# More tensor work released per unit in the second batch, a normalisation moved from VectorE to GpSimd, 7 instead of 14 leading products

## Chip, cores and metric

The kernel runs on one core of a Trainium2 chip. The metric is the device time of one execution in microseconds (us); the time of a kernel is the median of its runs. The core's engines run side by side and each works through its own list of instructions in order: TensorE (PE in the rows; PEld is its weight load), VectorE (DVE), ScalarE (ACT), GpSimd (POOL), and SyncE (SP), which here issues nearly all transfers.

## What is computed

Three layers in a row, on 2 batches of 576 tokens: attention with 8 heads of 64 that keeps, for each query, the 32 largest scores; a gated MLP; a mixture of 8 experts.

```python
scores = q @ k.T / 8                                   # per head, 576 x 576
attn = softmax(scores where >= 32nd largest) @ v       # -> x, 576 x 512 per batch
h = gelu(x @ w_in);  u, vv = halves(h)                 # 512 columns each
v_n = (vv - mean(vv)) / sqrt(var(vv) + 1e-6) * g_ln    # per token
x = x + (u * (w_sg @ v_n + b_sg)) @ w_out              # w_sg mixes the 576 tokens
# router: expert e of a token is the argmax of x @ w_gate, or the expert of the token before
out = p[e] * (relu(x @ w1[e]) @ w2[e])
```

The line that the change touches is `(vv - mean) / sqrt(var)`: one value normalisation per tile of tokens.

## The kernel before

**Units.** Attention works in units of 128 queries of one head (the 64 left over of a batch are paired into half as many units), 36 per batch, 72 in all. Line numbers are those of the profile. A unit is: scores on TensorE (L325) and their copy to `s_sb` on ScalarE (L328); on VectorE the 24 largest by segments (L354, L357, L359, the last 8 into `last`); a sign mask and its count on ScalarE (L365) and a product on GpSimd into `rest` (L369, L370), of which VectorE takes the next 8 (`next`, L371); the exponential on ScalarE (L367, with `nm` from GpSimd, L362); the mask on VectorE (L381) or, every second unit, on ScalarE and GpSimd (L378, L379); five transposes on TensorE (L393, `pt_ps`), their copy `pt` on ScalarE (L396); the product with v on TensorE (L401, `pv`), and after every fourth unit the division into the tile's `row` on VectorE (L406, L408, L417).

**The rest of the work** is cut into steps in a queue named `between`, each with an estimate in us. The function `pump` is called after each unit with a number from the table `RATE` (one entry per tile, 5 for each batch): it adds that number to a credit (at most 6) and takes steps off the queue, in order, while the credit lasts. Steps are: loading and decoding `w_in` (8 of 2.0, L196 to L204); per tile of tokens the MLP's input, 8.1 in all (L453 for u, L459 for v, L566 for the router's share); then for the first batch `spread` (20 in all, L541), `load_projection` (14; its first four steps are decoding of `w_out` and hold no product), `decide` (4.4) and `project` (14.4, L617). These last four, and the MLP of the tile shared by both batches, are queued when the second batch's first tile is done; the MLP of each tile of the second batch is queued behind them when that tile is done. When the last unit is done, `x_done` transposes the last tile (L439, copied to `xT` by ScalarE, L440), what is left on the queue is emptied, and the last tile's MLP, the second batch's `spread` (L523), the router and the experts follow.

**The order.** The kernel is written in a framework whose scheduler places every instruction by priority and by a model of time. Units have a high priority, so they run ahead of the queue's steps as far as buffers allow (7 of `s_sb`, 5 of `e_sb`). A change in the number or cost of instructions therefore moves others on all engines.

**The normalisation** (L470 to L477, once for each of 9 tiles): ScalarE writes the gelu of v into a `row` buffer (L466), VectorE takes its mean and variance (L470, L472) and adds 1e-6 (L474), GpSimd raises that to the power -0.5 (L476), and VectorE writes (v - mean) times that into `vn` (L477). Of the second batch's `vn`, ScalarE writes a high part and GpSimd the rest (L490, L491), both of which the products of L523 read.

**The start.** 14 products of constants (L821, `WARM`) that nothing reads lead TensorE's list, before the first scores.

Of the kernel before, what the change touches and what calls it, by code (L numbers as in the profile page):

```python
# [17 lines left out]
OP = mybir.AluOpType  # L18
# [4 lines left out]

WIDTHS = (224, 176, 160, 152, 152, 144, 136, 120)

RATE = (2.0, 2.0, 2.0, 2.0, 2.0, 2.4, 2.4, 2.4, 2.2, 2.2)

AHEAD = 2000
EVAC = 2000
# [7 lines left out]

FILL = (2, 2, 2, 3)

WARM = 14  # L40
KEEP = 30


# [1 line left out]
def tile_topk_gmlp_moe(  # L45
# [15 lines left out]
    nc = tc.nc  # L61
# [107 lines left out]
    def attention(fast):  # L169
# [76 lines left out]
        KK, QH, QL, V1, XB, XT, VN, UT, LG, DONE = {}, {}, {}, {}, {}, {}, {}, {}, {}, []  # L246

        def load_k(b, h):
            if PLAIN[b]:
                if h % 2 == 0:  # L250
                    KK[b, h] = kv.tile([P, S], F32R, name="kk", bufs=8).bitcast(F32)
                    nc.sync.dma_start(KK[b, h], kT[b, h:h + 2].rearrange("h d s -> (h d) s"))
                return
            kr = raw.tile([P, S], F32, name="kr")
            for s in range(2):
                nc.sync.dma_start(kr[s * D:(s + 1) * D], kT[b, h])
            KK[b, h] = kv.tile([P, S], F32R, name="kk", bufs=8)
            nc.scalar.activation(KK[b, h], kr, AF.Copy)
            nc.gpsimd.tensor_tensor(KK[b, h][D:], kr[D:], KK[b, h][D:].bitcast(F32), op=OP.subtract)
# [163 lines left out]
        def tile_of(b, j):  # L423
            return (b, j) if j < NJ - 1 else BOTH
# [17 lines left out]
        def mlp_in(t):  # L442
            b, j = t
            ps = {}

            def u(f):
                if f == 0:
                    if j == 0 or t == BOTH:
                        VN[b] = one.tile([P, 1 if t == BOTH else NJ - 1, F2], F32, name="vn2" if t == BOTH else "vn")
                        UT[b] = one.tile([P, CF, P if t == BOTH else FULL], F32, name="ut2" if t == BOTH else "ut")  # L450
                    ps["u"] = ps_m.tile([P, CF, P], F32, name="m_ps")
                for c in range(CD):
                    nc.tensor.matmul(ps["u"][:, f, :], w_in_sb[:, c, f * P:(f + 1) * P], XT[t][:, c, :], start=c == 0,  # L453
                                     stop=c == CD - 1)

            def v(c):
                if c == 0:
                    ps["v"] = ps_m.tile([P, F2], F32, name="m_ps")
                nc.tensor.matmul(ps["v"], XT[t][:, c, :], w_in_sb[:, c, F2:], start=c == 0, stop=c == CD - 1)  # L459
                if c < CD - 1:  # L460
                    return
                DONE.append(t)
                k = j % (NJ - 1)
                with tc.high_priority(offset=EVAC):
                    vg = one.tile([P, F2], F32, name="row", bufs=3)
                    gelu = nc.scalar.activation(vg, ps["v"], AF.Gelu_apprx_tanh)  # L466
                    with tc.issue_after(gelu.ins):
                        nc.scalar.activation(UT[b][:, :, k * P:(k + 1) * P], ps["u"], AF.Gelu_apprx_tanh)
                    st = sm.tile([P, 6], F32, name="st", bufs=3)
                    nc.vector.bn_stats(st, vg)  # L470
                    mv = sm.tile([P, 2], F32, name="mv", bufs=3)
                    nc.vector.bn_aggr(mv, st)  # L472
                    ve = sm.tile([P, 1], F32, name="ve", bufs=3)
                    nc.vector.tensor_scalar(ve, mv[:, 1:2], 1e-6, None, op0=OP.add)  # L474
                    rs = sm.tile([P, 1], F32, name="rs", bufs=3)
                    nc.gpsimd.tensor_tensor(rs, ve, neghalf, op=OP.pow)  # L476
                    nc.vector.tensor_scalar(VN[b][:, k, :], vg, mv[:, 0:1], rs, op0=OP.subtract, op1=OP.mult)  # L477

            return ([(0.9, partial(u, f)) for f in range(CF)] + [(0.9, partial(v, c)) for c in range(CD)]
                    + [(0.9, partial(logits_x, t))])  # L480

# [270 lines left out]
        def pump(us):  # L752
            credit[0] = min(credit[0] + us, 6.0)
            while between and credit[0] >= between[0][0]:
                cost, step = between.pop(0)
                credit[0] -= cost
                with tc.issue_after(BACK[-1].ins), tc.issue_after(EVACS[-1].ins):
                    step()

        def body(b, fast):  # L760
            for m, j in enumerate(TILES[b]):
# [3 lines left out]
                for i in range(n):  # L765
# [11 lines left out]
                    if fast and b + 1 < B and m == NJ - 1:  # L777
                        with tc.high_priority(offset=1):
                            for h in range(2 * i + 1, min(2 * i + 3, H)):
                                load_k(b + 1, h)  # L780
                    pump(RATE[b * NJ + m] if fast else 100.0)
                t = tile_of(b, j)
# [27 lines left out]
        def begin(b):  # L810
            for h in range(H):
                if h % 4 == 0:
                    load_q(b, TILES[b][0], h)
                load_k(b, h)
                if h == H - 1:
                    load_v(b)


        idle = ps_m.tile([P, 4, P], F32, name="m_ps")
        for m in range(WARM):  # L820
            nc.tensor.matmul(idle, ones, tri[:, None, :].to_broadcast([P, 4, P]), start=m == 0, stop=m == WARM - 1)  # L821
        begin(0)
# [336 lines left out]
```

## Time and profile before

| what | us |
|---|---|
| median of 3 runs | 582.87 (582.1 to 584.3) |
| the profiled execution, whole time | 582.34 |
| its span (first to last instruction) | 580.5 |
| TensorE busy | 521.7 (90%) |
| VectorE busy | 335.2 (58%) |
| ScalarE busy | 297.0 (51%) |
| GpSimd busy | 258.0 (44%) |

The profiled execution took 1.8 us more than its span and 0.5 us less than the median. Busy shares are means over stages with different limits: attention of the first batch runs to about 185 us, that of the second to 356 us, the experts from about 429 us to the end, and each stage has to be read by itself. In a row of the timeline the first number is the start, the second how long it took, both in us; what stands in brackets at a row's end is the idle time of the engine before it, and what ended it.

### The profile page before, as it was taken

To read this page: it belongs to the slowest core of one execution; us is meant where nothing else is said; L and a number is where in the kernel's file an instruction comes from. 1 tells how busy PE (TensorE), PEld (TensorE's weight loads), DVE (VectorE), ACT (ScalarE), POOL (GpSimd) and SP (SyncE) were. 2 spreads that over 40 slices of the span, in tenths; PEclk is the share of its full clock that TensorE was granted. 3 is DMA by queue.
4 is the path that set the end of the run, shared out by engine and by line. 5 is a ranking of instruction groups with operands and counts; after the bars stand their busy time and mean duration, and the time that the engine had idled before them with its cause. 6 is when DMAs were issued, how large, how long until landed. Compare 5 with 4: busy or idle time off the path is not lost. (4 is left out here: it accounts for less than half of the span.)

```text
span 580.5 us, 10259 instructions
## 1 busy us (share of the span) xinstructions
PE 521.7 (90%) x3414; PEld 442.7 (76%) x3414; DVE 335.2 (58%) x1626; ACT 297.0 (51%) x545; POOL 258.0 (44%) x382
## 2 busy tenths in 40 slices
PE   6566898989989799998999999989889999999993
PEld 3445686867868587887866787786579999999992
DVE  4789998969789798689998711266301111111110
ACT  3579888979787887479877432321010111011110
POOL 5497997657758475447676510520310101000010
PEclk9799899999999999999999999999999999999997
DMA  8962320000000000003101300002599997684000
GB/s 173 268 191 81 112 72 5 25 1 28 20 10 28 19 16 5 11 20 92 46 29 36 110 20 19 0 1 74 186 356 387 389 376 264 234 297 169 18 36 17
DMA packets 42609, 61.55 MB, mean 106 GB/s; under 512 B 14056, under 2 KB 18152, under 8 KB 42544
## 3 DMA queue, kind: packets, MB, share of 16 engines
q1 hardware_dynamic: 40880, 55.80, 29.5%
q0 software_dynamic: 1664, 4.97, 2.5%
q8 instruction: 30, 0.49, 0.4%
q14 instruction: 35, 0.29, 0.2%
HBM read 53.68 MB, written 7.33 MB: 105 GB/s over the span
## 5 line engine op out<-in xcount | busy, mean ns | idle before, releaser
L401 PE MATMUL pv<-v,pt 128*128 128x128 f32 (+1 forms) x720 | 104.7, 279 | 7.3 <-DVE row L417 4.8
L401 PEld LDWEIGHTS pv<-v,pt 128*128 128x128 f32 x720 | 96.2, 194 | 15.1 <-DVE row L417 5.5
L369 POOL TENSOR_TENSOR rest<-s_sb,sg 128x576 f32<-128x576 f32 x72 | 93.3, 1296 | 28.5 <-ACT sg L365 27.2
L325 PE MATMUL s_ps<-kk,qh 128*128 128x288 f32 x288 | 86.2, 423 | 16.0 <-ACT s_sb L328 15.0
L354 DVE MAX8 cand<-s_sb 128x8 f32<-128x72 f32 x576 | 88.7, 219 | 13.7 <-ACT s_sb L328 13.5
L393 PE MATMUL pt_ps<-ident,e_sb 128*128 128x128 f32 x360 | 68.1, 277 | 16.3 <-ACT pt L396 5.5
L995 PE MATMUL h_ps<-xw,w_sb 128*128 128x152 f32 (+6 forms) x512 | 76.5, 298 | 1.0 <-DMA w_sb<-in_w_dram 1.0
L1006 PE MATMUL y_ps<-hT,w_sb 128*128 128x152 f32 (+6 forms) x512 | 75.3, 299 | 0.9 <-DMA w_sb<-in_w_dram 0.9
L325 PEld LDWEIGHTS s_ps<-kk,qh 128*128 128x128 f32 x288 | 50.2, 194 | 31.3 <-ACT s_sb L328 21.4
L995 PEld LDWEIGHTS h_ps<-xw,w_sb 128*128 128x128 f32 x512 | 71.4, 190 | 1.3 <-ACT hT L998 1.3
L1006 PEld LDWEIGHTS y_ps<-hT,w_sb 128*128 128x128 f32 x512 | 71.0, 190 | 1.2 <-DMA w_sb<-in_w_dram 1.2
L396 ACT ACTIVATE pt<-pt_ps 128x640 f32<-128x640 f32 x72 | 50.3, 699 | 36.3 <-PE pt_ps L393 36.1
L998 ACT ACTIVATE hT<-h_ps 128x152 f32<-128x152 f32 (+6 forms) x32 | 9.7, 302 | 113.1 <-PE h_ps L995 109.9
L393 PEld LDWEIGHTS pt_ps<-ident,e_sb 128*128 128x128 f32 x360 | 45.2, 143 | 28.2 <-ACT pt L396 8.3
L365 ACT ACTIVATE sg<-s_sb,last 128x576 bf16<-128x576 f32 x72 | 55.6, 773 | 18.7 <-DVE last L357 15.4
L371 DVE MAX8 next<-rest 128x8 f32<-128x583 f32 x72 | 54.7, 759 | 8.2 <-POOL rest L370 8.0
L367 ACT ACTIVATE e_sb<-s_sb,nm 128x576 f32<-128x576 f32 x72 | 55.5, 772 | 1.9 <-POOL nm L362 1.7
L967 POOL DMA_INDIRECT out_dram<-orow,to x10 | 10.0, 999 | 103.1 <-ACT orow L966 48.3
L328 ACT ACTIVATE s_sb<-s_ps 128x576 f32<-128x576 f32 x72 | 46.3, 642 | 13.3 <-PE s_ps L325 12.8
L1000 DVE TENSOR_SCALAR hT<-h_ps 128x152 f32<-128x152 f32 (+6 forms) x32 | 10.3, 323 | 73.6 <-PE h_ps L995 68.6
L379 POOL TENSOR_TENSOR e_sb<-e_sb,mask 128x576 f32<-128x576 f32 x36 | 46.3, 1287 | 13.4 <-ACT e_sb L367 6.7
L1008 DVE COPY yT<-y_ps 128x152 f32<-128x152 f32 (+6 forms) x32 | 9.9, 323 | 64.2 <-PE y_ps L1006 64.2
(247 smaller groups left out, 827.2 us busy)
## 6 DMA issues: line engine op xcount, KB each, us to landing
w_sb<-in_w_dram SPq DMA_DIRECT2D x32, 1024.0 KB, 12.4
dbl<-in_w_in_dram SPq DMA_DIRECT2D x8, 512.0 KB, 4.5
kk<-in_kT_dram SPq DMA_DIRECT2D x8, 288.0 KB, 4.9
qh<-in_qT_dram SPq DMA_DIRECT2D x32, 64.0 KB, 2.4
v<-in_v_dram SPq DMA_DIRECT2D x8, 256.0 KB, 6.1
dbl<-in_w_out_dram SPq DMA_DIRECT2D x4, 512.0 KB, 3.7
xin<-row SPq DMA_DIRECT2D x8, 256.0 KB, 2.0
back<-xin SPq DMA_DIRECT2D x8, 256.0 KB, 2.6
```

What stands on the lines that cost most here:

```text
L325: nc.tensor.matmul(s_ps[:, n, :HS], w, k[:, n * HS:(n + 1) * HS], start=m == 0, stop=m == len(terms) - 1)
L328: EVACS.append(nc.scalar.activation(s_sb.rearrange("p (n s) -> p n s", n=2), s_ps[:, :, :HS], AF.Copy))
L354: nc.vector.max(cand[:, 8 * g:8 * g + 8], s_sb[:, g * w:(g + 1) * w])
L365: nc.scalar.activation(sg, s_sb, AF.Sign, bias=last8[:, un, 7:8], scale=-LESS, accum_out=cnt)
L367: nc.scalar.activation(e_sb, s_sb, AF.Exp, bias=nm, scale=scale)
L369: nc.gpsimd.tensor_tensor(below[:, :S], s_sb, sg, op=OP.mult)
L371: nc.vector.max(next8[:, un, :], below)
L393: tr = nc.tensor.transpose(pt_ps[:, t * P:(t + 1) * P], p_sb[:, k0:k0 + P], ident)
L396: nc.scalar.activation(pt.rearrange("p t q -> p (t q)"), pt_ps[:, :NJ * P], AF.Relu)
L401: nc.tensor.matmul(PV[b][:, i % g, :], pt[:, t, :], V1[b][:, t, w * i * (D + 1):w * i * (D + 1) + nv], start=t == 0, stop=t == NJ - 1)
L995: nc.tensor.matmul(hp[:, :W], w1_sb[:, c, f * P:(f + 1) * P], xw[:, c, at], start=c == 0, stop=c == CD - 1)
L1006: nc.tensor.matmul(yp[:, :W], w2_sb[:, f, c * P:(c + 1) * P], hT[:, f, :W], start=f == 0, stop=f == CE - 1)
```

## The change

```diff
-RATE = (2.0, 2.0, 2.0, 2.0, 2.0, 2.4, 2.4, 2.4, 2.2, 2.2)
+RATE = (2.0, 2.0, 2.0, 2.0, 2.0, 2.8, 2.8, 2.8, 2.6, 2.6)
-WARM = 14
+WARM = 7
                     nc.gpsimd.tensor_tensor(rs, ve, neghalf, op=OP.pow)
-                    nc.vector.tensor_scalar(VN[b][:, k, :], vg, mv[:, 0:1], rs, op0=OP.subtract, op1=OP.mult)
+                    nc.gpsimd.tensor_scalar(VN[b][:, k, :], vg, mv[:, 0:1], rs, op0=OP.subtract, op1=OP.mult)
```

The last five entries of `RATE` belong to the second batch. Seven products leave TensorE's list, and nine normalisations go from VectorE's list to GpSimd's. The scheduler then places everything anew; three places show it.

VectorE near the start, before: the rows from the last maximum of the second unit on. L199 and L200 decode a piece of `w_in` that a transfer brings into `dbl`.

```order
L357 MAX last<-cand 128x8
L199 TENSOR_SCALAR m_ps<-dbl 128x512
L359 MATCH_REPLACE cand<-ta,cand 128x64
L354 MAX cand<-s_sb 128x8 x4
L371 MAX next<-rest 128x8
L354 MAX cand<-s_sb 128x8 x4
L200 SCALAR_TENSOR_TENSOR m_ps<-dbl,m_ps 128x512
L357 MAX ta<-cand 128x8
L199 TENSOR_SCALAR m_ps<-dbl 128x512
L381 SCALAR_TENSOR_TENSOR e_sb<-s_sb,next,e_sb 128x576
```

The same place in the changed kernel:

```order
L357 MAX last<-cand 128x8
L359 MATCH_REPLACE cand<-ta,cand 128x64
L354 MAX cand<-s_sb 128x8 x4
L371 MAX next<-rest 128x8
L354 MAX cand<-s_sb 128x8 x2
L357 MAX ta<-cand 128x8
L354 MAX cand<-s_sb 128x8 x2
L381 SCALAR_TENSOR_TENSOR e_sb<-s_sb,next,e_sb 128x576
L199 TENSOR_SCALAR m_ps<-dbl 128x512
```

The first decoding step now stands behind the first unit's mask (L381) and all that leads to it, not ahead of it.

TensorE at the end of attention, before: the last unit's product with v (L401), and what follows to the first product of the second `spread` (L523).

```order
L459 MATMUL m_ps<-w_in_sb,xT 128x512 x2
L401 MATMUL pv<-v_1852,pt 128x128 x5
L566 MATMUL m_ps<-w_rt_sb,xT 128x90 x4
L453 MATMUL m_ps<-xT,w_in_sb 128x128 x12
L439 MATMUL m_ps<-ident,row 128x128 x2
L453 MATMUL m_ps<-xT,w_in_sb 128x128 x4
L459 MATMUL m_ps<-w_in_sb,xT 128x512 x4
L453 MATMUL m_ps<-xT,w_in_sb 128x128 x16
L459 MATMUL m_ps<-w_in_sb,xT 128x512 x4
L566 MATMUL m_ps<-w_rt_sb,xT 128x90 x8
L523 MATMUL m_ps<-s_sb,e_sb 128x288
```

The same place in the changed kernel:

```order
L393 MATMUL pt_ps<-ident,e_sb 128x128
L401 MATMUL pv<-v_1845,pt 128x128 x5
L439 MATMUL m_ps<-ident,row 128x128 x2
L453 MATMUL m_ps<-xT,w_in_sb 128x128 x16
L459 MATMUL m_ps<-w_in_sb,xT 128x512 x4
L566 MATMUL m_ps<-w_rt_sb,xT 128x90 x4
L523 MATMUL m_ps<-s_sb,e_sb 128x288
```

The MLP of the last tile but one (the first L453 x12 and x4, L459 x4 and half of L566) has gone to places between the last units, and nothing stands any more between the last transposes (L393), the last unit's product, the tile's transposes (L439) and the MLP that reads them.

GpSimd at the fifth normalisation, before:

```order
L476 TENSOR_TENSOR rs<-ve,neghalf 128x1
L379 TENSOR_TENSOR e_sb<-e_sb,mask 128x576
L362 TENSOR_SCALAR nm<-ta 128x1
L369 TENSOR_TENSOR rest<-s_sb,sg 128x576
L370 TENSOR_SCALAR rest<-order,cnts 128x7
```

The same place in the changed kernel:

```order
L476 TENSOR_TENSOR rs<-ve,neghalf 128x1
L379 TENSOR_TENSOR e_sb<-e_sb,mask 128x576
L477 TENSOR_SCALAR vn<-row,mv,rs 128x512
L362 TENSOR_SCALAR nm<-ta 128x1
L369 TENSOR_TENSOR rest<-s_sb,sg 128x576
L370 TENSOR_SCALAR rest<-order,cnts 128x7
```

The normalisation stands in the middle of two units' work on GpSimd: `nm`, which the exponential waits for, and `rest`, which VectorE waits for, are queued behind it.

## Rows read from the trace of the kernel before

**Rows 1.** The page: busy us, share of the span, instructions of each engine.

```profile
PE 521.7 (90%) x3414; PEld 442.7 (76%) x3414; DVE 335.2 (58%) x1626; ACT 297.0 (51%) x545; POOL 258.0 (44%) x382
```

**Rows 2.** Stretches: window, length, busy us (count) of PE, PEld, DVE, ACT, POOL; clock.

```profile
20.00:40.00 20.00, 13.42 (x65) 10.13 (x65) 18.10 (x102) 15.52 (x29) 12.54 (x20) 0.83 1.00 253
60.00:220.00 160.00, 141.71 (x939) 117.78 (x938) 138.33 (x723) 134.45 (x237) 113.38 (x165) 1.00 0.10 31
220.00:260.00 40.00, 40.00 (x221) 32.65 (x220) 31.61 (x139) 25.47 (x43) 17.83 (x28) 1.00 0.03 11
320.00:360.00 40.00, 40.00 (x273) 32.43 (x272) 15.38 (x46) 13.75 (x20) 9.97 (x11) 1.00 0.16 54
```

**Rows 3.** Timeline of TensorE and its weight loads at the start.

```profile
2.56 5.14 PE L821 MATMUL m_ps<-tri,ones 128*128 128x512 bf16 x14 [2.56 <-POOL none L136]
2.94 0.15 PEld L821 LDWEIGHTS <-ones 128*128 128x128 bf16 x1 [0.28 <-issue]
3.37 0.15 PEld L821 LDWEIGHTS <-ones 128*128 128x128 bf16 x1 [0.28 <-issue]
7.54 1.13 PE L325 MATMUL s_ps<-kk,qh 128*128 128x288 f32 x4
24.26 2.13 PE L325 MATMUL s_ps<-kk,qh 128*128 128x288 f32 x4
```

**Rows 4.** Transfers into kk, issued from 2 to 3 us: issue, landing.

```profile
L252 SPq DMA_DIRECT2D kk<-in_kT_dram x2: 432/510/587, 2.3 to 2.9; - x2
DMA to landing us min/median/max: 2.8/2.8/2.8
```

**Rows 5.** Timeline of VectorE around the first decoding steps.

```profile
18.42 0.69 DVE L199 TENSOR_SCALAR m_ps<-dbl 128x512 uint32<-128x512 uint32 x1 [3.32 <-DMA dbl<-in_w_in_dram]
20.96 0.68 DVE L200 SCALAR_TENSOR_TENSOR m_ps<-dbl,m_ps 128x512 uint32<-128x512 uint32 x1
21.69 0.68 DVE L199 TENSOR_SCALAR m_ps<-dbl 128x512 uint32<-128x512 uint32 x1
22.27 0.81 DVE L381 SCALAR_TENSOR_TENSOR e_sb<-s_sb,next,e_sb 128x576 f32<-128x576 f32 x1
```

**Rows 6.** VectorE's normalisations from 90 to 240 us, and one beside GpSimd.

```profile
L477 DVE TENSOR_SCALAR vn<-row,mv,rs 128x512 f32<-128x512 f32 x5 | 4.6, 910 | 0.0
...
97.56 1.71 DVE L477 TENSOR_SCALAR vn<-row,mv,rs 128x512 f32<-128x512 f32 x1
...
97.47 1.27 POOL L379 TENSOR_TENSOR e_sb<-e_sb,mask 128x576 f32<-128x576 f32 x1
```

**Rows 7.** GpSimd's groups: count, busy us, mean ns of one, idle before.

```profile
L204 POOL TENSOR_TENSOR w_in_sb<-w_in_sb,dbl 128x512 f32<-128x512 f32 x8 | 10.4, 1294 | 9.6 <-ACT dbl L203 9.6
...
L267 POOL MEMSET v<- 64x583 f32 x2 | 1.2, 577 | 0.0
```

**Rows 8.** Waits of TensorE from 206 to 320 us: total, times, longest.

```profile
PE pv L401 <- DVE row L417: 1.7, 2, 0.9
PE pt_ps L393 <- POOL rest L370: 1.7, 1, 1.7
...
PE pt_ps L393 <- ACT pt L396: 0.4, 1, 0.4
```

**Rows 9.** Timeline of the last unit and tile: TensorE, ScalarE, VectorE.

```profile
353.18 0.38 PE L393 MATMUL pt_ps<-ident,e_sb 128*128 128x128 f32 x2
...
355.12 1.28 PE L401 MATMUL pv<-v,pt 128*128 128x128 f32 x10
...
359.81 0.38 PE L439 MATMUL m_ps<-ident,row 128*128 128x128 f32 x2
...
353.66 0.70 ACT L396 ACTIVATE pt<-pt_ps 128x640 f32<-128x640 f32 x1 [4.46 <-PE pt_ps L393]
...
360.23 0.60 ACT L440 ACTIVATE xT<-m_ps 128x512 f32<-128x512 f32 x1 [3.82 <-PE m_ps L439]
...
356.97 0.42 DVE L417 TENSOR_TENSOR row<-pv,rc 128x256 f32<-128x256 f32 x1
```

## The prediction, on record before the changed kernel was timed

> **What bounds the kernel now.** I read the page's busy shares first: TensorE is busy for 521.7 of 580.5 us, so no change in the order can give back more than its 58.8 us of idle time [rows 1]. The windows then tell where that idle time lies, and it is not where the rates act. From 220 to 260 and from 320 to 360 us TensorE is busy all of the time (40.00 of 40.00) [rows 2]: in most of the second batch each tensor step that is taken earlier only pushes another one back. In the first batch nothing alone is the bound: from 60 to 220 us TensorE is busy 141.7 of 160 us, VectorE 138.3, ScalarE 134.5, GpSimd 113.4 [rows 2]; the engines wait for each other in turn. From 20 to 40 us VectorE is the bound, with 18.1 of 20 us against TensorE's 13.4 [rows 2]. So three questions are left: does VectorE get through the start sooner, does the first batch get faster with the normalisation on GpSimd, and does the second batch keep TensorE as full as before up to the second `spread`?
>
> **The change part by part.** All terms are against the profiled execution, 582.34 us, which lies 0.5 us under the median of 582.87.
>
> *Seven products fewer.* The first ones stand 0.43 us apart (2.94 to 3.37) [rows 3], so seven end by 2.56 + 7 x 0.43 = 5.6 us instead of 7.5. The keys for the first scores were issued at 2.3 us and landed 2.8 us later, at 5.1 [rows 4], so the scores can begin at 5.6, some 1.9 us earlier. That alone is worth nothing: VectorE comes to the first decoding step, L199, and sits idle for 3.32 us until its transfer lands at 18.42 [rows 5], and SyncE's list is the same up to that transfer. What is worth something is the order that goes with it. In the changed kernel L199 stands behind the first unit's mask L381, so that what VectorE did from 18.42 to the end of L381 at 23.08, less the three decoding steps within (0.69 + 0.68 + 0.68), now fills the wait: 4.66 - 2.05 = 2.6 us. VectorE being the bound there, I take -2.6; the ends are -3.3 (the whole wait) and 0 (another wait takes its place, see the rivals). The decoded piece itself is later by that much, and nothing reads it before the first MLP.
>
> *The normalisation, in the vector-bound part.* Five of the nine lie between 90 and 240 us and took VectorE 4.6 us, a mean of 0.91 us; one of them took 1.71 us while GpSimd ran a product of two tensors beside it [rows 6]. All five leave VectorE. GpSimd gets five operations of 512 elements per partition that it did not run before. A product of two tensors of that size takes it 1.29 us, and filling 583 elements 0.58 us [rows 7]; the new one reads one tensor and does two operations, so I put it at 0.8, with those two as its ends. Behind it stand `nm` and `rest`, for which ScalarE and VectorE wait. The ends for the whole are -4.6 us (all of VectorE's time returns, GpSimd has room) and +6.5 (five times 1.29 stand in the way and VectorE's time is hidden anyway). By the busy shares of rows 2 I let half of VectorE's gain count and a third of GpSimd's cost: -2.3 + 0.33 x 4.0 = -1.0. The trace shows the two engines in each other's way in row L477 at 97.56 [rows 6]; the Trainium skill's page "GPSIMD Engine Reference", section 8 (Key points), says that they share interfaces to SBUF and get in each other's way where VectorE uses both ports or reads two tensors, which agrees. Its section 3.1 measures 769 ns for a simple pass over 512 elements; by that figure, an estimate, the sum would hardly differ.
>
> *The rates, until the last units.* The second batch's first tile leaves 8.1 + 20 + 14 + 4.4 + 14.4 on the queue, and its next three tiles add 8.1 each: 85.2. From then on the 32 units grant 16 x 2.4 + 16 x 2.2 = 73.6 before, and 16 x 2.8 + 16 x 2.6 = 86.4 now, each plus at most 6 carried over. Where TensorE is full this moves no time. Between 206 and 320 us it does wait, five kinds of wait that come to 4.7 us with 1.7, 1.7 and 0.4 among them [rows 8], the longest in the units in which the queue holds the decoding of `w_out` and no product; with the higher rate these are 8 / 2.8 = 2.9 units instead of 3.3. I take -1.0 of that, with 0 and -4.7 as ends. The order also has two more table loads on ScalarE, among the last units, where ScalarE is busy for 13.75 of 40 us [rows 2]: they are hidden, and would show only if an exponential came too late for its unit, five units ahead as they run. The row transfers on SyncE move with their steps; the last loads of q still stand ahead of every wait for a projection, so nothing new is queued behind one.
>
> *The rates, behind the last unit.* Here the queue is now empty, and the MLP of the last tile but one no longer stands between the steps of a chain that it used to hide. In the new order TensorE meets three waits in a row: for the copy of the last transposes (they end at 353.18 + 0.38 = 353.56, the copy at 354.36: 0.8 us), for the division after the last product (355.12 + 1.28 = 356.40 to 356.97 + 0.42 = 357.39: 1.0 us) and for the copy of the transposed tile (359.81 + 0.38 = 360.19 to 360.83: 0.6 us) [rows 9]. Before, TensorE had other products for all three and waited for none (40.00 of 40.00) [rows 2]. They sum to 2.4, with the handovers 2.5 us. The work moved away takes as long where it is now, so this is a loss: +2.5, with +3.0 if the last normalisation, now on GpSimd, also comes late for `spread`, and 0 if something else fills in; the order shows nothing that could.
>
> Sum: -2.6 - 1.0 - 1.0 + 2.5 = -2.1 us. 582.34 - 2.1 = 580.2 against the profiled execution, and **580.8 us** against the median, 0.4% less.
>
> **The rivals.**
>
> *VectorE's time comes back in full.* If GpSimd, busy 113.4 of 160 us, takes the five normalisations into its gaps, the term is -4.6 instead of -1.0: 580.8 - 3.6 = 577.2. For it: the slow ones among the five were slow because of GpSimd, and that contention goes too. Against it: VectorE is not alone at the bound there. Chance 0.23.
>
> *The start gives nothing.* With seven products the clock may be granted at its lower level for longer. At the lower level (1.2 instead of 2.4 GHz) four score products took 2.13 us, at the higher 1.13 [rows 3], and from 20 to 40 us the mean grant was 0.83 [rows 2]. If the first six units' scores all run at the lower level, each 1.0 us longer, the sixth ends later than before in spite of the earlier start, and VectorE waits for scores instead of for the transfer. The first term is then 0: 583.4. Against it: TensorE is fed without a pause from 2.56 us on just as before, since scores follow the products. Chance 0.13.
>
> *Slower: GpSimd stands in the way.* Each of the five holds up `nm` and `rest` of a unit, VectorE and TensorE come to wait for `rest` and masks (one such wait was 1.7 us [rows 8]), and the drawn-out unit is not caught up. In full this is +6.5 instead of -1.0: 580.8 + 7.5 = 588.3; at three quarters of the 6.5, 586.7. It decides from six tenths on (581.8 + 3.9 = 585.7); below that the start's gain covers most of it. For it: the first batch is coupled, so a delay on the fourth engine can end last. The Trainium skill, "GPSIMD Engine Reference", section 4.1 (Engine selection), gives this rival a voice: elementwise work on a tile belongs on VectorE and not on GpSimd. No row before shows this operation on GpSimd. Chance 0.14.
>
> **How the numbers follow.** The forecast, 580.8 with its own range of 577.5 to 584, has 0.50. A change of under 0.5%, 2.9 us, cannot be told from none here, so the bounds are 580.0 and 585.8. About a third of the forecast's chance and all of the first rival's lie below: 0.41. Most of the last rival's and a little of the forecast's lie above: 0.15. The rest is 0.44. The range reaches from under the first rival to just past the point from which the slower one decides: 576 to 586.
>
> **What would show it.** In the changed profile VectorE's first L199 should stand after L381; it may still wait there, since VectorE starts 1.9 us earlier, up to 3.3 + 1.9 - 2.6 = 2.6 us; the 36th unit's product should end 2 to 5 us earlier. Nine normalisations should stand on GpSimd at 0.6 to 1.3 us each. TensorE should be full from about 210 us on and then wait three times, 2.5 us in all, between the last unit's transposes and the last tile's MLP. I am wrong if the first batch ends no earlier than before, if GpSimd's operation takes over 1.3 us, or if the waits behind the last unit are absent.

## The result, and the profile after

| | us |
|---|---|
| forecast | 580.8 (576 to 586) |
| the changed kernel, median of 14 runs | 585.6 (582.6 to 589.2) |
| the kernel before, median of 14 runs beside it | 582.5 (581.7 to 585.8) |
| ratio | 1.0051, interval 1.0030 to 1.0071 |
| profiled execution, changed kernel | 586.54, span 584.7 |

The change costs 3.0 us (0.0051 x 582.5). The time lies inside the range, but on the other side of the old time than the forecast. Page of the changed kernel, busy us, share of the span, instructions; it answers to [rows 1]:

```profile
PE 529.9 (91%) x3406; PEld 452.2 (77%) x3407; DVE 338.5 (58%) x1617; ACT 299.8 (51%) x547; POOL 279.3 (48%) x391
```

TensorE has seven products less and is busy 8.2 us longer: part of its work ran at the lower of its two clock levels. Stretches of the changed kernel (columns as in [rows 2]):

```profile
20.00:40.00 20.00, 15.45 (x67) 11.48 (x66) 18.46 (x99) 16.06 (x31) 14.72 (x20) 0.74 1.05 256
60.00:220.00 160.00, 143.72 (x949) 120.48 (x948) 140.93 (x729) 138.46 (x245) 124.34 (x172) 0.99 0.09 28
260.00:280.00 20.00, 15.17 (x89) 13.08 (x89) 15.60 (x72) 14.71 (x28) 11.41 (x15) 0.83 0.10 34
320.00:360.00 40.00, 39.70 (x262) 31.47 (x262) 15.74 (x48) 19.64 (x30) 17.57 (x15) 1.00 0.10 34
268.85:275.68 6.83, 6.26 (x24) 5.64 (x25) 6.63 (x37) 5.14 (x10) 4.57 (x6) 0.50 0.00 0
```

From 60 to 220 us TensorE is busier than before (143.7 against 141.7 us), which fits a faster first batch; the table below measures it. From 260 to 280 us it does 89 products; the kernel before does 126 there, at a clock of 1.00:

```profile
260.00:280.00 20.00, 17.40 (x126) 15.48 (x125) 19.07 (x91) 18.93 (x37) 15.45 (x22) 1.00 0.22 68
```

That is where the gain went, and a second piece of it went behind the last unit.

**How far ahead each kernel is.** To place gains and losses I give every product of TensorE the time that one of its line takes when they follow each other without a pause in the kernel before (0.243 us for L325, 0.11 for L393, L401 and L453, 0.43 for L459, and so on; the leading products count nothing), 485 us in all, and read from each trace when a given amount was done. The table gives that moment for the kernel before, and by how much the others are ahead (-) or behind (+). The kernels beside the changed one are those of the experiments below; they do the products in different orders, so steps of under 1 us mean nothing, and in the first batch, where the orders differ most, steps of under about 2 us. In the first 30 us of work the count jumps by up to 5 us from one amount to the next, so the table starts behind that.

| TensorE work done | before, at | changed | old rates (e1) | rates alone (e2) | seven alone (e3) | GpSimd alone (e4) | seven, 3 buffers (e10) |
|---|---|---|---|---|---|---|---|
| 40 us | 77.8 | -3.7 | -3.4 | +0.2 | -5.4 | +0.4 | -3.0 |
| 140 us | 192.7 | -6.9 | -6.5 | +0.2 | -3.4 | -2.9 | -6.0 |
| 160 us | 218.9 | -6.6 | -6.3 | +0.2 | -6.6 | -3.0 | -8.5 |
| 200 us | 258.9 | -6.6 | -6.3 | +0.4 | -5.0 | -3.0 | -6.9 |
| 220 us | 282.1 | +0.3 | -4.6 | +7.0 | -4.9 | -0.6 | -6.2 |
| 280 us | 344.2 | -0.7 | -5.1 | +6.1 | -6.5 | +0.6 | -8.2 |
| 320 us | 386.1 | +4.7 | -4.2 | +10.0 | -6.5 | +1.5 | -8.2 |
| 480 us | 565.4 | +4.1 | -3.8 | +10.0 | -7.9 | +1.1 | -8.5 |

Both kernels with the new rates fall back by about 7 us between 200 and 220 us of work, and by 4 to 5 us between 280 and 320. No other kernel of the table does either.

**The first loss: the decoding of w_out.** VectorE's first decoding step for the four pieces of `w_out`, before and then changed (in brackets the idle time ahead and what ended it):

```profile
256.60 0.69 DVE L199 TENSOR_SCALAR m_ps<-dbl 128x512 uint32<-128x512 uint32 x1
...
260.61 0.68 DVE L199 TENSOR_SCALAR m_ps<-dbl 128x512 uint32<-128x512 uint32 x1
...
265.08 0.69 DVE L199 TENSOR_SCALAR m_ps<-dbl 128x512 uint32<-128x512 uint32 x1
...
270.21 0.70 DVE L199 TENSOR_SCALAR m_ps<-dbl 128x512 uint32<-128x512 uint32 x1 [0.89 <-DMA dbl<-in_w_out_dram]
```

```profile
251.65 0.68 DVE L199 TENSOR_SCALAR m_ps<-dbl 128x512 uint32<-128x512 uint32 x1
...
252.79 0.71 DVE L199 TENSOR_SCALAR m_ps<-dbl 128x512 uint32<-128x512 uint32 x1
...
260.96 0.69 DVE L199 TENSOR_SCALAR m_ps<-dbl 128x512 uint32<-128x512 uint32 x1 [0.56 <-DMA dbl<-in_w_out_dram]
...
264.08 0.69 DVE L199 TENSOR_SCALAR m_ps<-dbl 128x512 uint32<-128x512 uint32 x1 [2.30 <-DMA dbl<-in_w_out_dram]
```

Before, they stand 4.0, 4.5 and 5.1 us apart. Now they come in pairs, 1.1 us apart, with 8.2 us between the pairs. A raw piece lives in one of two buffers `dbl`, which is free for the next transfer only when GpSimd has done L204 with it. In the changed kernel, GpSimd, ScalarE and TensorE show what follows:

```profile
255.37 3.08 POOL L204 TENSOR_TENSOR w_out_sb<-w_out_sb,dbl 128x512 f32<-128x512 f32 x2 [2.18 <-ACT dbl L203]
...
257.22 0.34 SPq L196 DMA_DIRECT2D dbl<-in_w_out_dram  x1
...
265.40 0.60 ACT L201 ACTIVATE w_out_sb<-m_ps 128x512 f32<-128x512 f32 x1 [2.39 <-DVE m_ps L200]
...
266.44 0.69 ACT L396 ACTIVATE pt<-pt_ps 128x640 f32<-128x640 f32 x1
...
267.18 0.77 PE L393 MATMUL pt_ps<-ident,e_sb 128*128 128x128 f32 x5 [1.98 <-ACT pt L396]
269.42 2.29 PE L325 MATMUL s_ps<-kk,qh 128*128 128x288 f32 x4 [1.47 <-ACT s_sb L328]
```

The third transfer is issued at 257.22, behind GpSimd's step for the first piece, and lands 3.7 us later. VectorE stands in order and waits 2.30 us for the fourth; ScalarE's L201 waits 2.39 us for VectorE; the copy `pt` of a unit is queued behind L201, and TensorE waits 1.98 us for it, then 1.47. From 268.85 us on, within the second of these waits, the granted clock is 0.50, the lower level (1.2 GHz), for 6.8 us: the four scores at 269.42 took 2.29 us, those at 264.06 took 1.14.

**The second loss: behind the last unit.** TensorE in the changed kernel:

```profile
364.55 1.38 PE L401 MATMUL pv<-v,pt 128*128 128x128 f32 x10 [0.85 <-ACT pt L396]
366.86 0.44 PE L439 MATMUL m_ps<-ident,row 128*128 128x128 f32 x2 [0.93 <-DVE row L417]
367.98 3.84 PE L453 MATMUL m_ps<-xT,w_in_sb 128*128 128x128 f32 x32 [0.69 <-ACT xT L440]
```

0.85 + 0.93 + 0.69 = 2.47 us, where the kernel before waits for none of the three. By the count of the table the place costs somewhat more than its idle time: 3.1 us between 298 and 310 us of work, where these waits lie. Another 1.6 us go from 314 to 318, where the clock is 0.50 from 384.9 to 388.3 us, behind a wait for VectorE that the kernel before has too (changed, then before):

```profile
384.23 0.40 PE L523 MATMUL m_ps<-s_sb,e_sb 128*128 128x288 f32 x1 [1.56 <-DVE ut L551]
```

```profile
381.01 0.40 PE L523 MATMUL m_ps<-s_sb,e_sb 128*128 128x288 f32 x1 [1.64 <-DVE ut L551]
```

Before, the clock is 1.00 there. Whether the three waits some 17 us earlier brought the fall is not shown: e2 and e5 below have the same three waits, the first of them longer (1.43 and 1.44), lose 3.7 us each from 298 to 310 us of work, and their clock does not fall in this stretch.

### The profile page after: what moved, and what is told of

It reads as the page before. It is cut to its first block, busy times and chain, and to the rows that moved or that the text cites. A ratio compares the mean times of both kernels' runs of the same rounds, so it can differ in the third digit from the quotient of the medians.

```text
span 584.7 us, 10239 instructions
## 1 busy us (share of the span) xinstructions
PE 529.9 (91%) x3406; PEld 452.2 (77%) x3407; DVE 338.5 (58%) x1617; ACT 299.8 (51%) x547; POOL 279.3 (48%) x391
## 5 line engine op out<-in xcount | busy, mean ns | idle before, releaser
L401 PE MATMUL pv<-v,pt 128*128 128x128 f32 (+1 forms) x720 | 107.7, 283 | 10.7 <-ACT pt L396 5.0
L401 PEld LDWEIGHTS pv<-v,pt 128*128 128x128 f32 x720 | 98.9, 198 | 18.9 <-ACT pt L396 7.8
L325 PE MATMUL s_ps<-kk,qh 128*128 128x288 f32 x288 | 90.2, 438 | 16.1 <-ACT s_sb L328 15.2
L393 PE MATMUL pt_ps<-ident,e_sb 128*128 128x128 f32 x360 | 71.2, 282 | 9.1 <-ACT pt L396 4.4
L325 PEld LDWEIGHTS s_ps<-kk,qh 128*128 128x128 f32 x288 | 52.0, 200 | 34.7 <-ACT s_sb L328 21.9
L995 PEld LDWEIGHTS h_ps<-xw,w_sb 128*128 128x128 f32 x512 | 72.6, 192 | 0.2
L371 DVE MAX8 next<-rest 128x8 f32<-128x583 f32 x72 | 54.9, 763 | 14.2 <-POOL rest L370 14.0
L393 PEld LDWEIGHTS pt_ps<-ident,e_sb 128*128 128x128 f32 x360 | 47.3, 147 | 18.2 <-issue 4.9
```

The lines of the kernel that those rows point to most:

```text
L325: nc.tensor.matmul(s_ps[:, n, :HS], w, k[:, n * HS:(n + 1) * HS], start=m == 0, stop=m == len(terms) - 1)
L371: nc.vector.max(next8[:, un, :], below)
L393: tr = nc.tensor.transpose(pt_ps[:, t * P:(t + 1) * P], p_sb[:, k0:k0 + P], ident)
L401: nc.tensor.matmul(PV[b][:, i % g, :], pt[:, t, :], V1[b][:, t, w * i * (D + 1):w * i * (D + 1) + nv], start=t == 0, stop=t == NJ - 1)
L995: nc.tensor.matmul(hp[:, :W], w1_sb[:, c, f * P:(f + 1) * P], xw[:, c, at], start=c == 0, stop=c == CD - 1)
```

## The experiments

Ratios are to the kernel before, run beside each; 0.01 is 5.8 us.

**Each part alone, and the rates taken back.**

e1, from the changed kernel:

```diff
-RATE = (2.0, 2.0, 2.0, 2.0, 2.0, 2.8, 2.8, 2.8, 2.6, 2.6)
+RATE = (2.0, 2.0, 2.0, 2.0, 2.0, 2.4, 2.4, 2.4, 2.2, 2.2)
```

> The changed kernel with the old rates (2.4 and 2.2 for the second batch), seven leading products and the normalisation on GpSimd. Theory A, the rates lost the time: in the changed profile the decoding steps of w_out come closer together than the two buffers behind them are refilled, TensorE waits 7 to 9 us more than before between 250 and 277 us (its lower clock counted in), and 2.5 us more behind the last unit; without the new rates the gain of the first batch (7.4 us at unit 42) stays and the kernel takes 576 to 578 us. Theory B, GpSimd's normalisation, 2.1 us each instead of VectorE's 0.5 to 1.7, lost the time: this kernel still has it and takes 584 us or more. Theory C, the scheduler's new order is as good or bad by chance in every variant: the time lies anywhere from 578 to 588 and the place of the loss is a new one.

Measured: 579.04 us, 0.9930 (0.9898 to 0.9962). Nearer to theory A; GpSimd's operation is still there and the kernel is 3.2 us faster than before, so theory B falls as the main cause. The time is above A's 576 to 578: see e3.

e2, from the kernel before, the opposite edit of that line (2.4 to 2.8, 2.2 to 2.6).

> The kernel before with the new rates alone (14 leading products, normalisation on VectorE). Theory A: no gain of the first batch, whole loss of the second: 588 us or more, with TensorE idle between 250 and 277 us and 2.5 us of waits behind the last unit. Theory B: the rates cost nothing but the 2.5 us behind the last unit, less the 1.0 us that a fuller queue gives: 582 to 585 us. Theory C: no loss at the place where the changed kernel has it.

Measured: 593.23 us, 1.0188 (1.0146 to 1.0231). The rates alone cost 11 us, and at the same two places. VectorE's L199 stand at 258.92, 260.06, 268.33 and 270.78 us, in pairs as in the changed kernel, and the three waits behind the last unit are 1.43, 0.93 and 0.69 us. Theory A holds, C falls.

e3, from the kernel before:

```diff
-WARM = 14
+WARM = 7
```

> The kernel before with seven leading products instead of 14 and nothing else changed. If the first batch's gain is the start's (the wait for the first decoding step filled, 2.6 us forecast): 580 us, unit 36 ends 2 to 3 us earlier. If the start's new order also saves what the changed kernel shows beyond that, unit 42 ends 7 us earlier and the time is 575 to 577 us. If the start gives nothing, because the lower clock lasts longer there: 582 to 584 us, and the first batch's gain was the normalisation's.

Measured: 575.35 us, 0.9867 (0.9838 to 0.9896): 7.7 us less from this one number, faster than both kernels. What VectorE waited for from 0 to 30 us (us in total, times, longest), before and then with seven products:

```profile
DVE cand L354 <- ACT s_sb L328: 6.7, 2, 6.4
DVE m_ps L199 <- DMA dbl<-in_w_in_dram: 3.3, 1, 3.3
```

```profile
DVE cand L354 <- ACT s_sb L328: 5.0, 1, 5.0
...
DVE m_ps L199 <- DMA dbl<-in_w_in_dram: 0.8, 1, 0.8
```

Both waits shrink, by 1.7 and by 2.5 us, 4.2 in all. But by the table the 5.4 us that e3 is ahead at 40 us of work have become 3.4 at 140, and 3.2 are won anew at the change of batches, where TensorE's waits (before from 188 to 214 us, seven products from 185 to 212) fall from 5.2 to 2.4 us:

```profile
PE pv L401 <- DVE row L417: 2.7, 2, 2.0
PE pv L401 <- ACT pt L396: 1.4, 1, 1.4
PE s_ps L325 <- ACT s_sb L328: 0.7, 1, 0.7
PE pt_ps L393 <- ACT pt L396: 0.4, 1, 0.4
```

```profile
PE pv L401 <- DVE row L417: 1.3, 2, 0.9
PE s_ps L325 <- ACT s_sb L328: 1.1, 1, 1.1
```

That second part is the scheduler's new placing; nothing in the start forces it, and no run here shows what does.

e4, from the kernel before:

```diff
-                    nc.vector.tensor_scalar(VN[b][:, k, :], vg, mv[:, 0:1], rs, op0=OP.subtract, op1=OP.mult)
+                    nc.gpsimd.tensor_scalar(VN[b][:, k, :], vg, mv[:, 0:1], rs, op0=OP.subtract, op1=OP.mult)
```

> The kernel before with the normalisation on GpSimd and nothing else changed. Theory A: the move is worth -1 to -4.6 us in the first batch, which the second batch keeps: 578 to 582 us. Theory B: nine operations of 2.1 us stand ahead of what VectorE and ScalarE wait for: 586 to 590 us, and the end of unit 42 is later than before. In either case GpSimd's L477 should take about 2.1 us, as in the changed kernel.

Measured: 583.03 us, 1.0003 (0.9984 to 1.0022), between the two theories: a gain of 2.9 us in the first batch, by the table, and a loss of 4.5 us between 200 and 320 us of work. GpSimd's group in it, mean ns in the column behind the bar:

```profile
L477 POOL TENSOR_SCALAR vn<-row,mv,rs 128x512 f32<-128x512 f32 x9 | 18.8, 2090 | 1.0
```

**Which of the two places, and why there.** e8 and e9, from the changed kernel, each with the new rate in part of the entries:

```diff
-RATE = (2.0, 2.0, 2.0, 2.0, 2.0, 2.8, 2.8, 2.8, 2.6, 2.6)
+RATE = (2.0, 2.0, 2.0, 2.0, 2.0, 2.4, 2.4, 2.4, 2.6, 2.6)   e8
+RATE = (2.0, 2.0, 2.0, 2.0, 2.0, 2.8, 2.8, 2.8, 2.2, 2.2)   e9
```

> The changed kernel with the new rate only in the first three entries of the second batch (2.8, 2.8, 2.8, 2.2, 2.2). VectorE's decoding steps of w_out then stand in pairs as in the changed kernel, and some products are left for the tail. Theory A1: nearly all of the loss is there, 583.5 to 586 us, with TensorE's waits of 0.5, 0.4, 1.4, 2.0 and 1.5 us at the decoding as in the changed kernel. Theory A2: 579 to 581 us.

Measured: 583.57 us, 1.0001 (0.9986 to 1.0017); against e1 that is 0.7%, 4.2 us. L199 stands in pairs again (249.79, 250.93, 259.27, 262.45). TensorE's waits there, from 240 to 275 us, first in e9 and then in e8, where the steps stand apart (248.78, 252.78, 257.20, 262.00):

```profile
PE pt_ps L393 <- ACT pt L396: 2.2, 1, 2.2
PE s_ps L325 <- ACT s_sb L328: 2.0, 2, 1.5
PE pv L401 <- ACT pt L396: 1.8, 2, 1.4
```

```profile
PE pt_ps L393 <- POOL rest L370: 1.8, 1, 1.8
PE pv L401 <- DVE row L417: 0.9, 1, 0.9
```

6.0 us with pairs, 2.7 without; and the clock was at its lower level for 6.8 us behind the waits of e9 (from 266.9), against 3.4 in e8 (from 263.2). The time is at the lower edge of what theory A1 gave for it; the changed kernel is 2.9 us slower still (1.0051 against 1.0001), which is what the last two entries add.

> The changed kernel with the new rate only in its last two entries (2.4, 2.4, 2.4, 2.6, 2.6). The decoding steps of w_out then stand on VectorE as far apart as in the kernel with the old rates (579.04 us), while the queue runs dry about as early as in the changed kernel: no product is left between the last unit's product and the transposes of its tile. Theory A1, the loss lies mostly at the decoding of w_out (by the traces +5.1 us between that place and 20 us of tensor work later) and less at the tail: 580.5 to 582.5 us, no waits of TensorE over 1 us there that the old rates did not have, 1.5 to 2.5 us of waits behind the last unit. Theory A2, the loss lies mostly at the tail: 584 us or more.

Measured: 583.15 us, 0.9989 (0.9967 to 1.0011), above A1's 582.5. The decoding is as forecast, and the waits behind the last unit are 1.09 + 0.69 = 1.8 us. What was not forecast is a third place: the router's step L646 of the first batch waits 3.59 us for VectorE, 0.4 us before and at most 0.7 in the others. TensorE, VectorE and GpSimd of e8:

```profile
311.04 0.38 PE L646 MATMUL m_ps<-ident,enc 128*5 128x128 f32 x1 [3.59 <-DVE enc L642]
```

```profile
308.42 1.21 DVE L669 TENSOR_SCALAR sx<-sx 128x5 f32<-128x5 f32 x1
...
309.68 1.30 DVE L642 TENSOR_TENSOR enc<-fm,fr 128x5 f32<-128x5 f32 x1
```

```profile
308.20 4.12 POOL L491 TENSOR_TENSOR v<-w_sg_sb,s_sb 128x576 fp32r<-128x576 f32 x3
```

Two operations on 5 elements took 1.21 and 1.30 us beside three of GpSimd's; in the kernel before they took 0.16 us each. So e8 does not give the price of the tail alone; by the same count as in the table it loses 2.2 us between 280 and 310 us of work.

e7, from the changed kernel (the second place where a `dbl` buffer is taken has the same edit):

```diff
-            hl = raw.tile([P, 2 * n], U32, name="dbl", bufs=2)
+            hl = raw.tile([P, 2 * n], U32, name="dbl", bufs=3)
```

> The changed kernel with three buffers behind the raw pieces (dbl) instead of two; rates, products and normalisation as changed. If two buffers are the cause at the decoding (the third transfer can only be issued when GpSimd is done with the first piece, and VectorE meets its L199 8 us after the second one), then the transfer is there in time, the waits of VectorE for dbl (2.9 us) go and with them most of TensorE's 5.7 us of waits there: 579 to 582 us, with the waits behind the last unit still there. If the cause is only that the steps are released too close, so that GpSimd, ScalarE and VectorE have too much of that work at once, it stays at 584 to 587 us.

Measured: 583.53 us, 1.0009 (0.9988 to 1.0030), 2.4 us less than the changed kernel. VectorE's four L199, with no wait for a transfer left:

```profile
259.34 0.68 DVE L199 TENSOR_SCALAR m_ps<-dbl 128x512 uint32<-128x512 uint32 x1
...
261.81 0.69 DVE L199 TENSOR_SCALAR m_ps<-dbl 128x512 uint32<-128x512 uint32 x1
...
264.97 0.68 DVE L199 TENSOR_SCALAR m_ps<-dbl 128x512 uint32<-128x512 uint32 x1
...
268.48 0.67 DVE L199 TENSOR_SCALAR m_ps<-dbl 128x512 uint32<-128x512 uint32 x1
```

Between 200 and 220 us of work e7 falls back by 1.9 us, like e1 (1.7), and not by 6.9: with a third buffer the first loss is nearly gone. This does not part the buffers from the place, though. The edit also moved the decoding: its first step stands behind the 59th unit's `next` (L371) on VectorE, in the changed kernel behind the 57th's. The time is nevertheless above the 579 to 582 expected, because e7 is only 4.4 us ahead at 200 us of work (the changed kernel 6.6; at 40 us the two are 3.1 and 3.7 ahead), and the tail's waits of 0.85, 0.93 and 0.69 us are all there.

**GpSimd's part, and the start.** e5 is the changed kernel with L477 back on VectorE, e13 the kernel with seven products and three buffers (e10, below) with L477 on GpSimd.

> The changed kernel with the normalisation back on VectorE: new rates and seven leading products alone. If GpSimd's 2.1 us operations are what made the changed kernel slower, this one comes to 579 us or less. If the rates are, it stays near the changed kernel's 585.6 us: 575.35 us of seven products alone plus the 6.5 to 11 us that the rates cost in the two pairs measured give 582 to 586 us, with VectorE again waiting some 3 us for pieces of w_out.

Measured: 585.99 us, 1.0044 (1.0018 to 1.0071): as slow without GpSimd's operation as with it. The rates cost 1.0044 / 0.9867, 10.4 us here. Where, its trace cannot tell: the profiled execution took 582.25 us, 3.7 less than the median.

> Seven leading products, three buffers dbl, old rates, and the normalisation on GpSimd: beside the kernel with three buffers and seven products (573.8 us) this gives the normalisation alone, beside the changed kernel with three buffers (583.5 us) the rates alone. If GpSimd's gain in the first batch (3 us) is lost again in the second, as in the two pairs measured so far: 574 to 577 us, and the rates are worth 6 to 9 us. If the third buffer takes the loss in the second batch away: 571 us.

Measured: 579.18 us, 0.9931 (0.9910 to 0.9951): beside e10 the normalisation costs 5.8 us, more than expected, and the rates, e7 against e13, 4.5 us, fewer. Nor is there a gain in the first batch here: by the count of the table e13 is 3.5 us ahead at 140 us of work and e10 6.0.

e11 has 12 leading products in the kernel before, e12 none (`WARM = 0`) and three buffers.

> The kernel before with 12 leading products instead of 14 and nothing else changed. Scores start 0.86 us earlier, and on VectorE the first decoding step L199 stands behind all that it stands behind with seven products but the mask L381. If it is the order that pays (1.8 us of work put into the wait) and the earlier start does not: tensor work is 1.8 us ahead at 30 us and the time is 580 to 581 us. If both pay, 2.7 us ahead and 579 to 580 us. If only the earlier start pays: 0.9 us ahead, 581.5 us.

Measured: 579.40 us, 0.9934 (0.9915 to 0.9953), which is the time given for both paying, but not for that reason. The earlier start did not come about in the profiled execution: the scores begin at 7.56 us (7.54 before).

```profile
2.57 5.16 PE L821 MATMUL m_ps<-tri,ones 128*128 128x512 bf16 x12 [2.57 <-POOL none L136]
7.56 1.14 PE L325 MATMUL s_ps<-kk,qh 128*128 128x288 f32 x4
```

Its twelve products stand 0.43 us apart to the last; of the fourteen before, the last four stand 0.21 apart. So e11 tries the order alone: VectorE's wait at the first L199 falls from 3.32 to 1.30 us (0.23 more at the second). By the count it is 1.5 us ahead at 40 us of work and 0.8 at 140; 3.8 us come at the change of batches, where TensorE's waits are 1.7 us instead of 5.2.

> The kernel before with no leading products at all and three buffers dbl. Beside the kernel with seven and three buffers (573.8 us): the keys land at 5.1 us, so the scores can start only 0.4 us earlier. If TensorE's clock at the start doesn't depend on the products: 572.5 to 574 us. If it does (TensorE idle until 5.1 us), the first units' scores run at the lower level, 2.1 instead of 1.1 us each, and the time is 576 us or more.

Measured: 583.09 us, 0.9994 (0.9977 to 1.0010): the gain is gone. TensorE's first scores in e12, and in e10 with seven products:

```profile
5.55 2.26 PE L325 MATMUL s_ps<-kk,qh 128*128 128x288 f32 x4 [5.55 <-DMA kk<-in_kT_dram]
8.55 2.29 PE L325 MATMUL s_ps<-kk,qh 128*128 128x288 f32 x4 [0.74 <-ACT s_sb L328]
```

```profile
2.56 3.15 PE L821 MATMUL m_ps<-tri,ones 128*128 128x512 bf16 x7 [2.56 <-POOL none L136]
5.50 1.99 PE L325 MATMUL s_ps<-kk,qh 128*128 128x288 f32 x4
8.23 1.24 PE L325 MATMUL s_ps<-kk,qh 128*128 128x288 f32 x4 [0.74 <-ACT s_sb L328]
```

Without leading products the first four units' scores take 2.3 us each; with seven only the first of these is slow. By the count of the table e12 is 0.3 us ahead at 40 us of work and e10 3.0, so products that nothing reads can account for 2.7 of the 9.3 us between the two. The rest comes later: e12 is 0.5 us ahead at 140 us of work and e10 6.0, and at the change of batches e12's waits are 4.9 us, about as before, and e10's 2.8. What in the start forces that, no run shows.

**The best version.** e10 is e3 with the third buffer of e7.

> The kernel before with seven leading products and three buffers behind the raw pieces (dbl); rates old, normalisation on VectorE. Two buffers cost little at the old rates: VectorE waited 0.9 us in all for pieces of w_out, and at the start it waits 0.8 us for the first piece, which the third buffer does not change. 573 to 575.5 us against the 575.35 of seven products alone. If the third buffer moves the order at the start for the worse, 577 us or more.

Measured: 573.80 us, 0.9832 (0.9811 to 0.9853): the fastest of all, 9.8 us under the kernel before.

## Why the prediction was wrong

| part | forecast | measured by pairs of kernels |
|---|---|---|
| seven products | -2.6 (-3.3 to 0) | -7.7 (e3), -4.3 (e1 against e4), -8.2 (e5 against e2) |
| normalisation on GpSimd | -1.0 (-4.6 to +6.5) | +0.2 (e4), +3.7 (e1 against e3), +0.4 (changed against e5), +5.8 (e13 against e10) |
| rates, both terms | +1.5 (-4.7 to +3.0) | +7.1 (changed against e1), +11.0 (e2), +10.4 (e5 against e3); with three buffers +4.5 (e7 against e13) |

By the intervals of its two ratios each of these is good to 1 to 3 us. One chain of them gives the result: -7.7 + 3.7 + 7.1 = +3.1 us.

**The step that failed is the rates until the last units,** where I took -1.0 with 0 as the worst. I saw the right place, "the units in which the queue holds the decoding of `w_out` and no product", and took a shorter stay in it for a gain. I had not asked whether the steps can go faster. They hardly can: before, the four pieces already followed at 4.0 to 5.1 us, with a wait of 0.89 us for a transfer, and took 13.6 us from the first L199 to the fourth; released faster, with two buffers, they took 12.4 (changed), 11.9 (e2) and 12.7 us (e9), with three 9.1 (e7). What the higher rate did was to bring them in pairs, which stood on three engines ahead of the units' own work. In place of -1.0 the runs show a loss there of 4.2 us (e9 against e1), nearly gone in e7. That two buffers are the whole cause stays open, since e7 moved the decoding as well.

**The rates behind the last unit** was right as a mechanism, and the idle time of the three waits named is 2.47 us for 2.5 forecast. The price is more than the idle time: by the count 3.1 us go around these waits, and from 280 to 320 us of work the changed kernel loses 5.4 us where e1 loses 0.9. The 3.4 us at the lower clock, in which 1.7 us of work were lost, are in that; the forecast had no term for them.

**The seven products** were about right at the place that the forecast named, and mis-sized for the whole kernel. L199 does stand behind L381, as read from the order, and VectorE's wait there is 1.46 us where I allowed up to 2.6. The second unit's `next`, before and then changed:

```profile
23.28 0.75 DVE L371 MAX8 next<-rest 128x8 f32<-128x583 f32 x1
```

```profile
19.57 0.75 DVE L371 MAX8 next<-rest 128x8 f32<-128x583 f32 x1
```

Three decoding steps were done by then before and one after, so of 3.7 us two steps of 0.68 go off: VectorE is at least 2.4 us ahead (2.7 in e3, where the row starts at 19.23), for 2.6 forecast. But the pairs give -4.3 to -8.2. The rest of the gain, in e3 3.2 us at the change of batches, was not to be read from the start; that it fell on the good side is luck, and it hid part of what the rates cost.

**The normalisation:** I put GpSimd's operation at 0.8 us with 1.29 as its upper end; it takes 2.09 (its group under e4; the same in the changed kernel), so the condition "if GpSimd's operation takes over 1.3 us" was met. Still the move gained 2.9 us in the first batch alone (e4), so the price of the operation was hidden there; with three buffers it was not (e13), and what it costs over the whole kernel changed from one order to the next, from +0.2 to +5.8 us.

**The rivals.** "GpSimd stands in the way" ended on the right side, but its mechanism is not what made the kernel slower: e5 has none of it and takes 586.0 us. At the old rates the move did cost 3.7 and 5.8 us beside seven products (e1, e13). "The start gives nothing" is refuted by e3. "VectorE's time comes back in full" comes nearer to the first batch than my -1.0 (e4 is 2.9 us ahead at 140 us of work, of the 4.6), but not to the kernel. The case that came, a higher rate that runs into the buffers of the loads it releases, was not among them.

## What to carry to other kernels

Before steps are released faster, look at the pace that they already keep: steps that feed on a small ring of buffers can hardly go faster than the ring, and released early they stand in order on several engines ahead of the work that matters. Where one line holds several numbers, try each alone; here one of the three parts was worth -7.7 us alone and another hid it. And where a scheduler places everything anew, a part's worth is what several pairs of kernels agree on, not one difference.

## What the runs showed of the hardware

- GpSimd's operation with two scalars per partition on 512 elements takes 2.09 us (nine times in each kernel that has it), longer than its product of two tensors of that size (1.29 us [rows 7]). The Trainium skill, "GPSIMD Engine Reference", section 3.1, has 769 ns for its best case, a tight loop over 512 elements; the measured value decides.
- VectorE's two operations on 5 elements in e8 did not run slower beside GpSimd, they were held: L669 from 308.42 to 309.63 us while GpSimd's first L491 ran from 308.20 to 309.61, and L642 to 310.99 while the second ran to 310.96. The Trainium skill, "SBUF — State Buffer", section "Who interferes with whom", describes that: the shared pair of ports is an exclusive lock for a whole instruction. The trace agrees.
- Waits of 1.98 and 1.47 us, 0.77 us of work between them, were followed by 6.8 us at the lower clock level in the changed kernel; with the rates old (e1) waits of 1.75 and 0.95 us at the same place were followed by 3.4 us, and in the kernel before waits of 1.66 and 0.94 us by none (clock 1.00 from 260 to 280 us).
- In the first 20 us of e12 the column of the granted clock says 1.00, while the scores take 2.26 to 2.29 us, as elsewhere at 0.50: at a kernel's start the durations tell more than that column.
